# Weight conversion in a retention + two-MLP kernel: and-or on VectorE replaced by a parametric ReLU on ScalarE

## The chip, the cores and the metric

The kernel runs on one core of a Trainium2 chip. The metric is the device time of one execution in microseconds (us). Engine names are those of the profile: PE is TensorE's matrix multiplication, PEld its weight load, DVE is VectorE, ACT is ScalarE, POOL is GpSimd, SP issues the transfers. L127 is line 127 of the kernel before.

## The reference

Three stages follow each other. The first is a decayed attention without softmax (retention): 4 batches, 8 heads, 576 tokens, 64 dims a head. Its result is laid out as x of 2304 tokens by 512. Two MLPs of width 2048 follow, with different activations:

```python
scores = scale * np.matmul(q, k.transpose(0, 1, 3, 2))
out = np.matmul(scores * Dmat, v)          # Dmat: gamma[h] ** (i - j) for i >= j
h = np.maximum(x @ moe_w_in, 0.0)
x = h * h @ moe_w_out
h = x @ moe2_w_in
out = (h * np.clip(h + 3.0, 0.0, 6.0) / 6.0) @ moe2_w_out
```

The q, k, v are float32; the weights (512 x 2048 and 2048 x 512, twice) reach the kernel as the bits of float64 numbers, so that the kernel has to make float32 of them.

## The kernel before

**Numbers.** Each operand of the MLPs' products is held in two float32r parts, a high one and the rest, and a product is three matmuls: high times high, rest times high, high times rest.

**Weights.** A step of an MLP takes 128 of the 2048 inner columns, f = 0 to 15. Its weights are two halves, (f, 0) of w_in and (f, 1) of w_out, each a tile of 128 partitions by 512 float64. A half goes through four functions. `load_w` brings the raw words. `scale_w` is two ACT instructions: L109 multiplies the high word, read as a float32, by 2^-112, L110 multiplies the low word by 2^-29 and rounds it to an integer. `narrow_w` makes the float32 of them: L124 shifts the scaled high word three bits to the left (DVE), L125 puts back the sign bit, which the shift has lost (one DVE instruction that ands and ors), L127 adds the low word as an integer. L127 runs on DVE, but on POOL for the second halves of the second MLP. `split_w` makes the two parts: a rounding copy, L138 on ACT or L136 on DVE (`on_dve`), and a subtraction on POOL, L139.

**Steps.** `h_part` computes h for one block of tokens and one f: 12 matmuls (L296) into a PSUM tile `hp`, then the activation, then the two parts of g. In the first MLP ACT takes the ReLU of `hp` into r (L306); the square is ACT's L308 in block 0 and DVE's L310 (r times r) in the other blocks. The high part of g is ACT's L316 in block 0, DVE's L318 elsewhere; the rest is DVE's L319. In the second MLP the activation is L312 on ACT and L313 on DVE, which reads `hp` again. `a_part` adds g's product with w_out to the block's PSUM accumulators (L340 in the first MLP, L342 in the second) and evicts them after f = 15 (L363 DVE, L365 ACT). On PE the order is h of step i+1, then the retention's matmuls of step i, then a of step i. `hp` has two buffers.

**Order.** The order of each engine's instructions is written out by hand, and each engine takes them in that order. Blocks of the first MLP have 512, 384, 512, 384, 512 tokens, those of the second 384, 512, 512, 512, 384. First comes the retention of the first block's four chunks of 128 tokens, with the first weights between them. During block 0 every step narrows half (f+1, 1), splits half (f+2, 0) with ACT and half (f+1, 1) with DVE, computes h of f+1, narrows (f+3, 0) and scales two more halves on ACT. A chunk of the next block's retention is spread over four steps of every block of the first MLP but the last: `prep_chunk` (POOL L190), `scores` (PE L204, DVE L210), `values` (PE, DVE L246, ACT L249, POOL L250) and `states` (PE, DVE L276, POOL L277). The second MLP's 32 halves are converted from step 4 of the last block of the first MLP to the 15th of the second MLP's first block, one half a step, and two halves in each of five of these steps; scaling is done two steps ahead of splitting, narrowing one. In f = 8 to 11 of the block before, `load_x1` reads a second-MLP block's input (DVE L384, POOL L385).

Of the kernel before, what the change touches and what calls it, by code (L numbers as in the profile page):

```python
# [9 lines left out]
F32 = mybir.dt.float32  # L10
# [4 lines left out]
AF = mybir.ActivationFunctionType  # L15
ALU = mybir.AluOpType

P = 128
B, H, S, D = 4, 8, 576, 64
# [6 lines left out]
NCHUNK = NT // P  # L26
# Blocks of tokens of the first MLP and of the second, with the buffer that each one's input is in.
BLOCKS = (
# [3 lines left out]

# Columns of the table of constants.
VD0 = 0
# [6 lines left out]
def constants():  # L41
    """Decay factors and causal masks, by the shapes alone.

    Within a chunk of 128 tokens gamma^(i-j) / sqrt(D) is (gamma^(i+1) / sqrt(D)) for the query
    i times gamma^-(j+1) for the key j; the state of the chunks before takes gamma^128 a chunk.
    """
    gamma = 1.0 - 2.0 ** (-5.0 - np.arange(H, dtype=np.float64))
    t = np.arange(P, dtype=np.float64)
    c = np.zeros((P, NCONST), np.float64)
    for p in range(NPAIR):  # L50
        for e in range(2):
            g = gamma[2 * p + e]
            c[64 * e : 64 * e + 64, QD0 + p * P : QD0 + (p + 1) * P] = g ** (t + 1) / np.sqrt(D)
            c[64 * e : 64 * e + 64, GC0 + p] = g**P
    c[:, VD0 : VD0 + H] = gamma[None, :] ** -(t[:, None] + 1)
    causal = t[:, None] <= t[None, :]
    half = (t[:, None] < 64) == (t[None, :] < 64)
    c[:, MK0 : MK0 + P] = causal
    c[:, MK0 + P : MK0 + 2 * P] = causal & half
    return c.astype(np.float32)  # L60
# [3 lines left out]
def retention_moe_kernel(ctx: ExitStack, tc, qk, kv, w1, w2, cst, out):  # L64
    """qk [18, 128, 2, 512]: per chunk of 128 tokens q and k, by (head pair's dims; pair, token).
    kv [18, 128, 2, 512]: per chunk k and v, by (token; head, dim).
    w1, w2 [16, 128, 1024]: per 128 of d_ff w_in (dim within c; c, ff) and w_out (ff; dim), the
    64 bits of float64 numbers.
    """
    nc = tc.nc  # L70
# [19 lines left out]

# [1 line left out]
    raws = {}  # L92
    wts = {}

    def load_w(ph, f, halves=(0, 1)):
        """The raw numbers, into the room that their two parts will have, which is as large."""
        src = (w1, w2)[ph].bitcast(I32)
        for i in halves:
            t = wpool.tile([P, DM, 2], I32, tag=f"w{f}_{i}", name=f"raw_{ph}_{f}_{i}")
            nc.sync.dma_start(  # L100
                t, src[f, :, 2 * DM * i : 2 * DM * (i + 1)].rearrange("p (n t) -> p n t", t=2)
            )
            raws[ph, f, i] = t

    def scale_w(ph, f, halves=(0, 1)):
        for i in halves:
            raw = raws[ph, f, i]
            low, high = raw[:, :, 0], raw[:, :, 1]
            nc.scalar.activation(high.bitcast(F32), high.bitcast(F32), AF.Copy, scale=2.0**-112)  # L109
            nc.scalar.activation(low, low.bitcast(U32), AF.Copy, scale=2.0**-29)  # L110

    def narrow_w(ph, f, halves=(0, 1)):
        """float64 bits to float32, rounded to nearest.

        The high word, times 2^-112 as a float32, has its exponent rebased: three bits to the left
        it is the float32 truncated to 20 bits of fraction, but for the sign. The low word's top
        bits, rounded, are added to the word as an integer.
        """
        for i in halves:
            raw = raws.pop((ph, f, i))  # L120
            low, high = raw[:, :, 0], raw[:, :, 1]
            t = stg.tile([P, DM], F32, tag="wt", name=f"wt_{ph}_{f}_{i}")
            ti = t.bitcast(I32)
            nc.vector.tensor_scalar(ti, high, 3, None, ALU.logical_shift_left)  # L124
            nc.vector.scalar_tensor_tensor(ti, high, -(2**31), ti, ALU.bitwise_and, ALU.bitwise_or)  # L125
            eng = nc.gpsimd if ph and i else nc.vector
            eng.tensor_tensor(ti, ti, low, ALU.add)  # L127
            wts[ph, f, i] = t

    def split_w(ph, f, halves=(0, 1), on_dve=False):  # L130
        """float32 into two float32r parts."""
        for i in halves:
            t = wts[ph, f, i]
            w = wpool.tile([P, 2, DM], F32R, tag=f"w{f}_{i}", name=f"w_{ph}_{f}_{i}")
            if on_dve:
                nc.vector.tensor_copy(w[:, 0, :], t)  # L136
            else:
                nc.scalar.activation(w[:, 0, :], t, AF.Copy)  # L138
            nc.gpsimd.tensor_tensor(w[:, 1, :], t, w[:, 0, :].bitcast(F32), ALU.subtract)  # L139
            wts[ph, f, i] = w  # L140

# [1 line left out]
    con = apool.tile([P, NCONST], F32, tag="con", name="con")  # L143
# [3 lines left out]
    state = [apool.tile([P, NPAIR, P], F32, tag=f"s{i}", name=f"state{i}") for i in range(2)]  # L147

    # k by the head pair's dims, one head's at a time, with noughts in place of the other head's.
    # While the weights are not all there, two more chunks have room in their place.  # L150
    kts = [apool.tile([P, 2, NPAIR, P], F32, tag=f"kt{i}", name=f"kt{i}") for i in range(2)]
# [31 lines left out]
    def where(c):  # L183
        """Fresh: a batch begins with the chunk. Straddle: one ends in its middle."""
        t0 = c * P
        return t0 % S == 0, t0 // S != (t0 + P - 1) // S, (t0 + P) % S == 0
# [91 lines left out]

# [1 line left out]
    x1 = dpool.tile([P, NC, NT], F32, tag="x1", name="x1")  # L280
# [4 lines left out]
    def h_part(ph, blk, f):  # L285
# [4 lines left out]
        order = [(c, wi, xi) for wi, xi in ((0, 0), (1, 0), (0, 1)) for c in range(NC)]  # L290
        # The first half of the first block's tokens is there before the second.
        parts = 2 if ph == blk == f == 0 else 1
# [11 lines left out]
        r = r[:, :nb]  # L304
        if ph == 0:
            nc.scalar.activation(r, hp[:, :nb], AF.Relu)  # L306
            if blk == 0:
                nc.scalar.activation(r, r, AF.Square)  # L308
            else:
                nc.vector.tensor_tensor(r, r, r, ALU.mult)  # L310
        else:
            nc.scalar.activation(r, hp[:, :nb], AF.Relu, bias=con3)  # L312
            nc.vector.scalar_tensor_tensor(r, r, 6.0, hp[:, :nb], ALU.min, ALU.mult)  # L313
# [72 lines left out]

# [1 line left out]
    for t in state:  # L388
# [51 lines left out]

    # The second MLP's weights are split over the steps of two blocks, as the first one's make room.
    todo = {}
# [89 lines left out]
```

## Time and profile before

| | before |
|---|---|
| timed runs, us | 928.20, 926.77, 928.01 (median 928.01) |
| span of the profiled execution, first to last instruction | 924.4 us |
| instructions | 11741 |
| PE busy | 891.0 us, 96% of the span |
| DVE busy, instructions | 499.9 us, 772 |
| ACT busy, instructions | 240.3 us, 411 |
| POOL busy, instructions | 205.9 us, 169 |

The profiled execution has no time of its own beside its span; the median of the runs is 3.6 us longer than the span, which is what lies around the first and last instruction. Busy time of an engine is the union of its instructions' times. A PE that is busy is not at its full rate, since matmuls that wait for an operand inside a group stretch; the rate is read from the starts of groups of twelve matmuls.

### The profile page before, as it was taken

How to read it: one execution, taken by the hardware profiler on the slowest of the kernel's cores; microseconds unless marked ns; L12 is line 12 of the kernel's file. 1: busy time of each engine (PE TensorE's matmuls, PEld its weight loads, DVE VectorE, ACT ScalarE, POOL GpSimd, SP SyncE). 2: the span in 40 equal slices, each digit the busy share in tenths (PEclk: the TensorE clock that was granted, in tenths of full speed). 3: DMA queues.
4: the chain of work that ended last, by engine and by line, in shares of the span. 5: the costliest groups of instructions: out<-in, count | busy, mean ns of one | idle time of the engine just before them, and what ended most of it. 6: DMA issues, size and time to landing. Idle time of an engine off the chain costs nothing.

```text
span 924.4 us, 11741 instructions
## 1 busy us (share of the span) xinstructions
PE 891.0 (96%) x4716; PEld 760.1 (82%) x4716; DVE 499.9 (54%) x772; ACT 240.3 (26%) x411; POOL 205.9 (22%) x169
## 2 busy tenths in 40 slices
PE   7899999999999999999999997899999999999998
PEld 6677768999888899998877786788888888888997
DVE  5899995433433334433889899633343334333333
ACT  2666662111111111112444553211111111111111
POOL 5555551110101001120356356300100110010000
PEclk9899999999999999999999999999999999999999
DMA  8934511121201111105565300100020002000100
GB/s 287 364 100 155 206 46 46 46 69 47 80 23 46 46 46 46 46 1 166 202 215 169 126 0 12 59 11 1 12 80 1 12 0 72 1 9 0 46 1 35
DMA packets 26549, 67.73 MB, mean 73 GB/s; under 512 B 3200, under 2 KB 5376, under 8 KB 26496
## 3 DMA queue, kind: packets, MB, share of 16 engines
q1 hardware_dynamic: 26496, 67.00, 21.2%
q8 instruction: 37, 0.61, 0.3%
q14 instruction: 16, 0.13, 0.0%
HBM read 57.55 MB, written 9.44 MB: 72 GB/s over the span
## 4 chain that ended last, share of the span: by engine, by line
PE 72%; DVE 17%; DMA 5%; issue 3%; ACT 2%; POOL 1%; SPq 1%; DVEq 0%; ACTq 0%; POOLq 0%
PE h L296 33%; PE acc L342 18%; PE acc L340 15%; DVE wt L127 4%; DVE wt L125 4%; DVE wt L124 3%; DVE g L319 2%; PE sc L204 2%; DMA raw<-w_dram 2%; DVE g L318 2%; DMA kt<-qk_dram 1%; PE o L223 1%; PE o L233 1%; ACT r L306 1%; DVE r L313 1%
## 5 line engine op out<-in xcount | busy, mean ns | idle before, releaser
L296 PE MATMUL h<-x,w 128*128 128x512 f32 (+2 forms) x1932 | 425.9, 368 | 5.3 <-ACT w L138 3.0
L296 PEld LDWEIGHTS h<-x,w 128*128 128x128 f32 x1932 | 352.3, 188 | 57.7 <-POOL w L139 5.7
L340 PE MATMUL acc<-g,w 128*128 128x512 f32 (+1 forms) x960 | 217.2, 373 | 5.1 <-POOL w L139 1.8
L342 PE MATMUL acc<-w,g 128*128 128x512 f32 x864 | 212.8, 393 | 9.1 <-DVE g L318 8.2
L342 PEld LDWEIGHTS acc<-w,g 128*128 128x128 f32 x864 | 160.8, 188 | 46.1 <-DVE g L318 9.8
L340 PEld LDWEIGHTS acc<-g,w 128*128 128x128 f32 x960 | 172.0, 188 | 31.6 <-POOL w L139 3.9
L313 DVE SCALAR_TENSOR_TENSOR r<-r,h 128x512 f32<-128x512 f32 (+1 forms) x80 | 50.7, 633 | 202.9 <-ACT r L312 202.9
L310 DVE TENSOR_TENSOR r<-r 128x384 f32<-128x384 f32 (+1 forms) x64 | 42.3, 662 | 173.0 <-ACT r L306 172.9
L312 ACT ACTIVATE r<-h,con 128x512 f32<-128x512 f32 (+1 forms) x80 | 51.5, 644 | 283.0 <-PE h L296 274.4
L319 DVE TENSOR_TENSOR g<-r,g 128x512 fp32r<-128x512 f32 (+1 forms) x160 | 120.7, 754 | 6.3 <-ACT g L316 1.3
L139 POOL TENSOR_TENSOR w<-wt,w 128x512 fp32r<-128x512 f32 x64 | 96.4, 1510 | 82.3 <-ACT w L138 48.8
L306 ACT ACTIVATE r<-h 128x512 f32<-128x512 f32 (+1 forms) x80 | 44.1, 551 | 240.5 <-PE h L296 231.4
L318 DVE CAST g<-r 128x512 fp32r<-128x512 f32 (+1 forms) x144 | 71.6, 497 | 14.3
L385 POOL TENSOR_TENSOR x<-x1r,x 128x512 fp32r<-128x512 f32 (+1 forms) x20 | 25.4, 1271 | 240.1 <-DVE x L384 238.4
L250 POOL TENSOR_TENSOR x<-x,x 128x512 fp32r<-128x512 f32 (+1 forms) x19 | 23.6, 1245 | 208.7 <-ACT x L249 208.7
L125 DVE SCALAR_TENSOR_TENSOR wt<-raw,wt 128x512 int32<-128x512 int32 x64 | 58.3, 911 | 2.2
L138 ACT ACTIVATE w<-wt 128x512 fp32r<-128x512 f32 x48 | 30.3, 631 | 87.4 <-DVE wt L127 53.4
L127 DVE CUSTOM_DVE_ANT_0 wt<-raw,wt 128x1024 uint16<-128x1024 uint16 x48 | 46.9, 977 | 3.5
L204 PE MATMUL sc<-q,kt 128*128 128x128 f32 x288 | 38.0, 285 | 5.8 <-POOL kt L392 4.2
L204 PEld LDWEIGHTS sc<-q,kt 128*128 128x128 f32 x288 | 36.4, 199 | 7.4 <-POOL kt L392 4.2
L109 ACT ACTIVATE raw<-raw 128x512 f32<-128x512 f32 x64 | 42.5, 663 | 0.0
L110 ACT ACTIVATE raw<-raw 128x512 int32<-128x512 uint32 x64 | 42.4, 662 | 0.0
(33 smaller groups left out, 325.0 us busy)
## 6 DMA issues: line engine op xcount, KB each, us to landing
raw<-w_dram SPq DMA_DIRECT2D x64, 512.0 KB, 6.0
kv<-kv_dram SPq DMA_DIRECT2D x14, 512.0 KB, 3.2
q<-qk_dram SPq DMA_DIRECT2D x18, 256.0 KB, 2.9
kt<-qk_dram SPq DMA_DIRECT2D x36, 128.0 KB, 3.1
out_dram<-ev SPq DMA_DIRECT2D x18, 256.0 KB, 2.3
x<-ev SPq DMA_DIRECT2D x12, 256.0 KB, 2.1
x1r<-x SPq DMA_DIRECT2D x12, 256.0 KB, 3.5
kv<-kv_dram SPq DMA_DIRECT2D x8, 256.0 KB, 5.4
```

Source lines behind the costliest of these rows:

```text
L125: nc.vector.scalar_tensor_tensor(ti, high, -(2**31), ti, ALU.bitwise_and, ALU.bitwise_or)
L127: eng.tensor_tensor(ti, ti, low, ALU.add)
L139: nc.gpsimd.tensor_tensor(w[:, 1, :], t, w[:, 0, :].bitcast(F32), ALU.subtract)
L204: nc.tensor.matmul(sc[e][:, p, :], kt[:, e, p, :], q[:, p, :], start=True, stop=True)
L296: nc.tensor.matmul(hp[:, ts], w[:, wi, c * P : (c + 1) * P], x[:, xi, c, ts], start=k == 0, stop=k == 3 * NC - 1,)
L306: nc.scalar.activation(r, hp[:, :nb], AF.Relu)
L312: nc.scalar.activation(r, hp[:, :nb], AF.Relu, bias=con3)
L313: nc.vector.scalar_tensor_tensor(r, r, 6.0, hp[:, :nb], ALU.min, ALU.mult)
L318: nc.vector.tensor_copy(g[:, 0, :nb], r)
L319: nc.vector.tensor_tensor(g[:, 1, :nb], r, g[:, 0, :nb].bitcast(F32), ALU.subtract)
L340: nc.tensor.matmul(acc[d][:, :nb], wt[:, sl], gt, start=first, stop=stop)
L342: nc.tensor.matmul(acc[d], gt[:, sl], wt, start=first, stop=stop)
```

## The change

The multiplication of the high word on ACT becomes a parametric ReLU with the same scale and a slope of -(2^32) for negative numbers. A negative word comes out positive with an exponent that is 32 higher, and the shift by three carries that bit to the sign's place. L125 goes. The integer addition is on DVE in all 64 conversions. In the first MLP r becomes the ReLU times `hp`, on DVE, in all five blocks. The comments are taken out, with empty lines in their place.

```diff
-            nc.scalar.activation(high.bitcast(F32), high.bitcast(F32), AF.Copy, scale=2.0**-112)
+            high = high.bitcast(F32)
+            nc.scalar.activation(high, high, AF.Prelu, scale=2.0**-112, alpha=-(2.0**32))
             nc.scalar.activation(low, low.bitcast(U32), AF.Copy, scale=2.0**-29)
...
             nc.vector.tensor_scalar(ti, high, 3, None, ALU.logical_shift_left)
-            nc.vector.scalar_tensor_tensor(ti, high, -(2**31), ti, ALU.bitwise_and, ALU.bitwise_or)
-            eng = nc.gpsimd if ph and i else nc.vector
-            eng.tensor_tensor(ti, ti, low, ALU.add)
+            nc.vector.tensor_tensor(ti, ti, low, ALU.add)
...
             nc.scalar.activation(r, hp[:, :nb], AF.Relu)
-            if blk == 0:
-                nc.scalar.activation(r, r, AF.Square)
-            else:
-                nc.vector.tensor_tensor(r, r, r, ALU.mult)
+            nc.vector.tensor_tensor(r, r, hp[:, :nb], ALU.mult)
```

## Rows read from the trace of the kernel before

**Rows 1.** The page's second part: busy tenths of PE and DVE in 40 equal slices of the span (23.1 us each).

```profile
PE   7899999999999999999999997899999999999998
DVE  5899995433433334433889899633343334333333
```

**Rows 2.** Busy time by stage: block 0 of the first MLP, and the stretch in which the second MLP's weights are converted. Columns: stretch, its length, busy us (and instructions) of PE, PEld, DVE, ACT, POOL, then granted clock, DMA share, GB/s.

```profile
45.00:139.00 94.00, 89.48 (x477) 68.81 (x476) 90.08 (x119) 59.25 (x102) 51.53 (x36) 1.00 0.37 128
480.00:591.00 111.00, 96.23 (x437) 79.17 (x436) 102.77 (x130) 50.46 (x90) 60.82 (x43) 0.98 0.23 75
```

**Rows 3.** PE's timeline where nothing holds it up (start us, us, what): three steps of block 1, which carry one chunk of retention between them, and one step without; a step of 512 tokens of the first MLP; a step of 384 tokens of the second.

```profile
152.80 2.24 PE L296 MATMUL h<-x,w 128*128 128x384 f32 x12
...
170.04 2.24 PE L296 MATMUL h<-x,w 128*128 128x384 f32 x12
...
174.20 2.24 PE L296 MATMUL h<-x,w 128*128 128x384 f32 x12
...
430.58 2.88 PE L296 MATMUL h<-x,w 128*128 128x512 f32 x12
...
436.02 2.88 PE L296 MATMUL h<-x,w 128*128 128x512 f32 x12
...
525.90 2.27 PE L296 MATMUL h<-x,w 128*128 128x384 f32 x12
...
530.08 2.27 PE L296 MATMUL h<-x,w 128*128 128x384 f32 x12
```

**Rows 4.** PE's timeline at the ends of the two stretches: a of block 0's first step, h of block 1's first step; h of step 12 of the first MLP's last block, h of the second MLP's second block, first step.

```profile
38.66 3.02 PE L340 MATMUL acc<-g,w 128*128 128x512 f32 x12 [0.74 <-ACT g L316]
...
143.74 2.27 PE L296 MATMUL h<-x,w 128*128 128x384 f32 x12
...
479.54 2.88 PE L296 MATMUL h<-x,w 128*128 128x512 f32 x12
...
590.44 2.88 PE L296 MATMUL h<-x,w 128*128 128x512 f32 x12
```

**Rows 5.** Instructions grouped by line from 45 to 139 us. Columns: line, engine, operation, output<-inputs, shapes, count | busy us, mean ns | idle of the engine before them.

```profile
L127 DVE CUSTOM_DVE_ANT_0 wt<-raw,wt 128x1024 uint16<-128x1024 uint16 x26 | 29.9, 1152 | 2.3
L125 DVE SCALAR_TENSOR_TENSOR wt<-raw,wt 128x512 int32<-128x512 int32 x26 | 23.8, 916 | 0.9
L124 DVE TENSOR_SCALAR wt<-raw 128x512 int32<-128x512 int32 x26 | 17.4, 668 | 0.1
```

**Rows 6.** The same view from 480 to 591 us.

```profile
L125 DVE SCALAR_TENSOR_TENSOR wt<-raw,wt 128x512 int32<-128x512 int32 x24 | 21.6, 898 | 0.8
L319 DVE TENSOR_TENSOR g<-r,g 128x384 fp32r<-128x384 f32 x15 | 19.2, 1280 | 0.5
L127 POOL TENSOR_TENSOR wt<-wt,raw 128x512 int32<-128x512 int32 x12 | 16.9, 1404 | 19.9 <-DVE wt L125 16.6 <-issue 3.4
L124 DVE TENSOR_SCALAR wt<-raw 128x512 int32<-128x512 int32 x23 | 15.1, 655 | 0.0
L318 DVE CAST g<-r 128x384 fp32r<-128x384 f32 x16 | 12.6, 790 | 1.6
L127 DVE CUSTOM_DVE_ANT_0 wt<-raw,wt 128x1024 uint16<-128x1024 uint16 x12 | 8.3, 692 | 0.4
```

**Rows 7.** What these operations take where POOL doesn't work beside them: two lines of the view of one source line (duration ns min/median/max), two instructions of the last block from the timeline, and two groups over the whole span.

```profile
L124 DVE TENSOR_SCALAR wt<-raw x64: 410/420/1524, 19.1 to 585.6; 128x512 int32<-128x512 int32 x64
...
L125 DVE SCALAR_TENSOR_TENSOR wt<-raw,wt x64: 691/693/1781, 19.6 to 586.1; 128x512 int32<-128x512 int32 x64
...
909.56 0.36 DVE L318 CAST g<-r 128x384 fp32r<-128x384 f32 x1
...
909.95 0.56 DVE L319 TENSOR_TENSOR g<-r,g 128x384 fp32r<-128x384 f32 x1
...
L310 DVE TENSOR_TENSOR r<-r 128x384 f32<-128x384 f32 x32 | 17.9, 558 | 91.7 <-ACT r L306 91.7
...
L313 DVE SCALAR_TENSOR_TENSOR r<-r,h 128x384 f32<-128x384 f32 x32 | 17.6, 551 | 44.0 <-ACT r L312 44.0
```

**Rows 8.** The timeline of one step of block 0.

```profile
78.67 1.48 POOL L139 TENSOR_TENSOR w<-wt,w 128x512 fp32r<-128x512 f32 x1 [2.02 <-ACT w L138]
...
79.13 1.56 DVE L127 CUSTOM_DVE_ANT_0 wt<-raw,wt 128x1024 uint16<-128x1024 uint16 x1
...
79.78 0.63 ACT L316 ACTIVATE g<-r 128x512 fp32r<-128x512 f32 x1
...
81.08 0.68 DVE L319 TENSOR_TENSOR g<-r,g 128x512 fp32r<-128x512 f32 x1
```

**Rows 9.** The timeline of the first 32 us: the last DVE instruction of the first conversion, PE's wait for the retention's state, the first matmuls of the MLP.

```profile
21.13 1.54 DVE L127 CUSTOM_DVE_ANT_0 wt<-raw,wt 128x1024 uint16<-128x1024 uint16 x1
...
26.35 1.12 PE L223 MATMUL o<-p,kv 128*64 128x128 f32 x8 [3.31 <-DVE state L276]
...
31.82 6.11 PE L296 MATMUL h<-x,w 128*128 128x256 f32 x36
```

**Rows 10.** Busy time in two short stretches (columns as in Rows 2; the granted clock is the first figure behind the last bracket).

```profile
26.00:28.00 2.00, 1.65 (x11) 1.35 (x11) 1.90 (x4) 0.66 (x2) 1.26 (x2) 0.50 1.02 407
586.00:588.00 2.00, 2.00 (x8) 2.00 (x7) 0.74 (x2) 0.00 (x0) 1.15 (x1) 0.50 0.00 0
```

**Rows 11.** The only table load of the whole span, in the view by line.

```profile
L243 ACT ACT_TABLE_LOAD x1 | 1.3, 1283 | 0.7 <-PEq L521 0.7
```

## The prediction

> **What bounds the kernel now.** I read the page's slices first [rows 1]. PE is at 9 in nearly all of them; the slices below 9 are the first two and those around slices 22 to 25, and there DVE is at 8 or 9. Everywhere else DVE is at 3 to 5. So the time is PE's own work plus what DVE takes from it in three places: the start, block 0, and the conversion of the second MLP's weights. The view by stage [rows 2] confirms it: DVE is busy 90.1 of 94 us in block 0 and 102.8 of 111 us in the second stretch, while ACT has 59 and 50 and POOL 52 and 61.
>
> PE's busy share hides the loss, so I take it from starts of matmul groups [rows 3]. Undisturbed, a 512-token step of the first MLP takes 436.02 - 430.58 = 5.44 us (2.72 for h, as much for a), a step of 384 tokens of the second 530.08 - 525.90 = 4.18, one of the first MLP 174.20 - 170.04 = 4.16. A chunk of retention adds (170.04 - 152.80) - 3 x 4.16 = 4.8 us. Block 0, from its first a to block 1's first h, holds 31 halves of a step and three chunks: 31 x 2.72 + 3 x 4.8 = 98.6 us. It takes 143.74 - 38.66 = 105.1 [rows 4], so 6.5 us are lost. From 479.54 to 590.44 there are four steps of 5.44, the change of blocks (h of 384 tokens, half of 4.16, and a of 512: 2.08 + 2.72) and fifteen steps of 4.18: 89.3 us. It takes 110.9; 21.6 us are lost. These two sums are the most that each stretch can give back.
>
> A second thing sets DVE's pace. In [rows 8] L127 begins at 79.13, while POOL's L139 runs from 78.67 to 80.15, and takes 1.56 us; the same operation takes 0.69 in the other stretch, where it never meets one [rows 6]. L124 has a minimum of 0.41 and a maximum of 1.52, L125 0.69 and 1.78 [rows 7]. A DVE instruction that works on SBUF alone waits until POOL's is done. The excess over the undisturbed time in block 0 is 26 x (1.152 - 0.692) = 12.0 us for L127, 26 x (0.916 - 0.693) = 5.8 for L125 and 26 x (0.668 - 0.42) = 6.4 for L124 [rows 5, 7]: 24 us for 51.5 us of POOL's work, 0.47 us for each. In the second stretch L125, L124, L318 and L319 give 4.9 + 5.4 + 6.9 + 10.8 = 28 us [rows 6, 7] for 60.8, or 0.46. So an instruction taken from POOL gives DVE nearly half of its time back.
>
> **The change, part by part.**
>
> *L125 away, everywhere.* Each costs DVE 0.69 us; the wait for POOL that it may have held passes to the next instruction, and I count that as not saved.
>
> *The addition for sixteen halves moves from POOL to DVE.* Twelve lie in the second stretch. DVE takes 12 x 0.692 = 8.3 us more; POOL loses 16.9 us [rows 6], which at 0.46 returns 7.8 us of waits. With L125 gone (24 x 0.69 = 16.6) DVE's demand there falls by 16.6 - 8.3 + 7.8 = 16 us, and it sets the pace for nearly the whole stretch. Its 111 us would become 95, still above PE's 89.3. Bounds of the gain: all of PE's loss, 21.6, above, and 6 below, if the waits remain that come from two halves or an input piece in one step. I take 14, a little under DVE's own 16: in the three steps with two halves DVE still needs more than 4.18 us (0.55 + 0.36 + 0.56 for the activation, 2 x 1.1 for the conversions, 0.46 x 2 x 1.4 of waits: 5.0). The conversion's path to PE also loses POOL's 1.4 us and one change of engine before L138.
>
> *Block 0: L125 away, the square moved to DVE.* From 45 to 139 us DVE loses 26 x 0.69 = 17.9 us and gains 13 multiplications (26 conversions are 13 steps). These read PSUM and SBUF like L313, which at 384 columns takes 0.551 against 0.558 for L310, which reads SBUF alone [rows 7]; so 0.69 at 512, 9.0 together, and no wait for POOL. Net -8.9 us. But r now goes ACT, DVE, ACT, DVE where it stayed on ACT for three instructions: DVE's next instruction is L319, and it waits for L316, 0.63 us on ACT [rows 8] and some 0.1 us of signalling. Nothing stands between them in DVE's order, so DVE stands still 0.7 us a step, 13 x 0.7 = 9.1 us. Behind it wait the next conversion's L124 and the retention's L210, L246 and L276; behind L316 on ACT wait four scalings and the next L138. Bounds: if the standstill falls into time in which POOL's L139 would have held up L124 anyway (6.4 us of such waits), DVE falls to some 94 - 8.9 + 2.7 = 88 us, which is PE's share of these 94 us (98.6 x 94 / 105.1 = 88.2), and all 6.5 us come back; if it adds in full, 94 - 8.9 + 9.1 = 94, and nothing does. I take the middle, 3.5. The next bound then is PE in steps with retention and ACT's order in the others.
>
> [...]
>
> *Blocks 1 to 4 of the first MLP.* L310 reads `hp` in place of r: the same time, PE hides it (DVE at 3 to 4 tenths, rows 1). `hp` is freed after DVE's instruction instead of ACT's; PE's next use of that buffer comes after a, which needs that DVE result anyway. Nothing.
>
> *The start.* DVE's instructions between 19 and 31 us are in one queue with the retention: PE waits 3.31 us for the state at 26.35, behind the first conversion, whose L127 runs till 22.67, and begins h at 31.82 [rows 9]. Two L125 stand ahead of that h, each between 0.69 and 1.78 us. PE also runs at half its clock behind that wait (0.50 from 26 to 28 us, rows 10), so a shorter wait may save a little more. Bounds 0 and 4 us; I take 2.5, two L125 at a mid value.
>
> *The parametric ReLU itself.* The trace has none. I take it to cost what the multiplication cost; ACT has 35 of 94 us free in block 0, and loses the square. That it costs more, by a table load, is the first rival.
>
> Sum: 2.5 + 3.5 + 14 = 20 us off the span of 924.4, so 904.4; with the 3.6 us around it 908.0, against the median of 928.01.
>
> **Rivals.**
>
> *Table loads (slower).* If the parametric ReLU lies in another table set than the copy beside it, ACT loads a table before and after each: 1.283 us [rows 11]. Place: `scale_w`, two halves a step in block 0, so four loads, 5.1 us. The 94 us hold 13 steps (26 conversions), of 7.2 us, and ACT is busy for 59.25 / 13 = 4.6 of them; less the square and with the loads it is 9.1: 1.9 us a step over now, 28 in fifteen. In the second stretch 24 x 2 x 1.283 = 62 us come to ACT's 50, about its length: nothing gained. With some 5 us at the start 928 + 33 = 961. It decides from two loads a step on, where ACT (4.0 + 2.6) passes PE's 98.6 / 15.5 = 6.4 us. For it: only one load in the whole span shows, and no such function. Against: that one load serves ReLU, square and copy together. Chance 0.05.
>
> [...]
>
> *The round trip costs more than it frees (slower).* In block 0, if each standstill also sets L319 behind a POOL instruction (0.87 as in rows 8) and L316's lateness delays L138 and so PE's next weights by 0.6, a step has 0.69 + 0.7 + 0.87 + 0.6 - 1.38 = 1.5 us more: 22 us, against 16.5 gained elsewhere: 933. It decides from 1.1 us a step. DVE's fullness speaks for it; against it, POOL's L139 for the DVE-split half runs just during the standstill. Chance 0.05.
>
> *A milder form of it.* Half a microsecond a step, +7.5 in place of -3.5: 919, still faster. Chance 0.14.
>
> *The second stretch keeps its waits.* The steps with two halves or an input piece lose what they lose now, and 6 us come back: 916. For it: DVE's order is fixed, and most PE waits sit in such steps. Chance 0.15.
>
> *Both of the last two and no gain at the start.* 928 + 7.5 - 6, less if PE's clock falls after a longer wait as it did at 586 us [rows 10]: about no change. Chance 0.04.
>
> **Numbers.** Forecast 908.0, chance 0.57, its own range 901 to 915. Faster by over 0.2% (what a measurement of this kernel can tell from none): 0.57 + 0.14 + 0.15 = 0.86; the same 0.04; slower 0.10. With every bound at its best the time is 928 - 4 - 6.5 - 21.6 = 896; I cut that to 900, since the three don't come together, and reach up to 921 to hold the two milder rivals.
>
> **What would show it.** L125 is gone and DVE's count falls by 64 - 16 - 16 = 32. From 480 us on, the second stretch shortens from 110.9 to about 97 us and DVE is no longer full in single steps; block 0 takes about 101.5, with DVE idle before L319 some 0.7 us, ended by ACT's L316; h begins near 29.5. It is wrong if ACT shows more than one table load, if block 0 takes more than 105, or if PE still waits over 10 us for L318 and w after 480 us.

## The result and the profile after

The changed kernel takes 901.61 us (median of four runs, 900.91 to 902.37). The kernel before, with one more run beside it, takes 927.53 (926.77 to 928.20): 25.9 us less, where the forecast was 20 less and 908.0. The ratio on record is 0.9726, 95% interval 0.9712 to 0.974 (the two medians alone give 0.972).

The first parts of the page after, instruction counts and slices of 22.5 us (compare rows 1):

```profile
span 898.8 us, 11669 instructions
PE 882.0 (98%) x4716; PEld 760.8 (85%) x4716; DVE 455.5 (51%) x740; ACT 229.8 (26%) x395; POOL 174.2 (19%) x153
...
PE   7899999999999999999999999999999999999998
...
DVE  4888884343343343443679899433333333333333
```

DVE has 32 instructions fewer and is busy for 455.5 us where it was for 499.9, ACT for 229.8 (240.3), POOL for 174.2 (205.9). PE's slices below 9 around the second MLP's weights have gone. DVE is still at 8 or 9 in slices 2 to 6 and 22 to 25, the same two places.

Some lines move in the new file: the high word's scaling is L110 (was L109), the shift L126 (L124), ReLU times `hp` L307, the high part of g L313 on ACT (L316) and L315 on DVE (L318), its rest L316 (L319), `a_part` L337 and L339 (L340, L342), the second MLP's activation L309 and L310.

PE's timeline after, at the ends of the stages (start us, us, what; compare rows 4): first a of block 0, first h of block 1, h of step 12 of the first MLP's last block, first h of the second MLP's second block.

```profile
36.93 2.94 PE L337 MATMUL acc<-g,w 128*128 128x512 f32 x12
...
134.91 2.27 PE L296 MATMUL h<-x,w 128*128 128x384 f32 x12
...
470.71 2.88 PE L296 MATMUL h<-x,w 128*128 128x512 f32 x12
...
564.77 2.88 PE L296 MATMUL h<-x,w 128*128 128x512 f32 x12
```

The differences between such starts give the stages. Block 0 is 134.91 - 36.93 = 98.0 us where it was 105.1, the second stretch 564.77 - 470.71 = 94.1 where it was 110.9, and the first a comes 1.7 us earlier: 7.1 + 16.8 + 1.7 = 25.6, the whole difference of the spans (924.4 - 898.8). Between the two stretches (335.8 us) and after the second (334.0) nothing changed.

Busy time in both stretches after (columns as in rows 2):

```profile
43.00:132.00 89.00, 87.21 (x478) 69.94 (x477) 75.14 (x107) 53.56 (x95) 46.49 (x36) 1.00 0.42 147
470.00:565.00 95.00, 92.33 (x441) 79.45 (x439) 85.06 (x119) 51.40 (x90) 40.55 (x31) 1.00 0.27 90
```

DVE has fallen from 96% of block 0 to 75.1 of 89 us, and from 102.8 of 111 to 85.1 of 95. The table loads that a rival feared did not come; over the whole span the view by line has one, as before, and the parametric ReLU takes what the scaled copy took (first line: the scaled copy in the kernel before, whole span; then two lines after):

```profile
L109 ACT ACTIVATE raw<-raw 128x512 f32<-128x512 f32 x64 | 42.5, 663 | 0.0
...
L110 ACT ACTIVATE raw<-raw 128x512 f32<-128x512 f32 x64 | 42.5, 664 | 0.0
...
L243 ACT ACT_TABLE_LOAD x1 | 1.3, 1283 | 0.7 <-PEq L518 0.7
```

### The profile page after: what moved, and what is told of

Same layout as the page of the kernel before. It is cut to its first block, busy times and chain, and to the rows that moved or that the text cites. A ratio compares the mean times of both kernels' runs of the same rounds, so it can differ in the third digit from the quotient of the medians.

```text
span 898.8 us, 11669 instructions
## 1 busy us (share of the span) xinstructions
PE 882.0 (98%) x4716; PEld 760.8 (85%) x4716; DVE 455.5 (51%) x740; ACT 229.8 (26%) x395; POOL 174.2 (19%) x153
## 4 chain that ended last, share of the span: by engine, by line
PE 82%; DMA 6%; DVE 5%; issue 3%; ACT 1%; POOL 1%; SPq 1%; DVEq 0%; POOLq 0%; ACTq 0%
PE h L296 38%; PE acc L339 20%; PE acc L337 18%; PE sc L204 2%; DMA raw<-w_dram 2%; DMA kv<-kv_dram 2%; PE o L223 2%; PE o L233 2%; DVE g L315 1%; DVE wt L127 1%; POOL w L139 1%; DVE wt L126 1%; DMA q<-qk_dram 1%; PE st L262 1%; DVE r L307 1%
## 5 line engine op out<-in xcount | busy, mean ns | idle before, releaser
L337 PE MATMUL acc<-g,w 128*128 128x512 f32 (+1 forms) x960 | 214.8, 372 | 0.0
L339 PE MATMUL acc<-w,g 128*128 128x512 f32 x864 | 210.9, 391 | 1.5 <-DVE g L315 1.5
L337 PEld LDWEIGHTS acc<-g,w 128*128 128x128 f32 x960 | 172.7, 188 | 22.7 <-ACT g L313 0.2
L339 PEld LDWEIGHTS acc<-w,g 128*128 128x128 f32 x864 | 161.1, 188 | 35.7 <-DVE g L315 2.6
L310 DVE SCALAR_TENSOR_TENSOR r<-r,h 128x512 f32<-128x512 f32 (+1 forms) x80 | 50.8, 634 | 203.0 <-ACT r L309 203.0
L307 DVE TENSOR_TENSOR r<-r,h 128x512 f32<-128x512 f32 (+1 forms) x80 | 50.6, 633 | 177.7 <-ACT r L306 177.6
L316 DVE TENSOR_TENSOR g<-r,g 128x512 fp32r<-128x512 f32 (+1 forms) x160 | 123.6, 772 | 16.2 <-ACT g L313 11.2
L309 ACT ACTIVATE r<-h,con 128x512 f32<-128x512 f32 (+1 forms) x80 | 51.7, 647 | 295.2 <-PE h L296 283.6
L139 POOL TENSOR_TENSOR w<-wt,w 128x512 fp32r<-128x512 f32 x64 | 88.3, 1386 | 125.4 <-ACT w L138 100.0
L306 ACT ACTIVATE r<-h 128x512 f32<-128x512 f32 (+1 forms) x80 | 44.3, 553 | 249.4 <-PE h L296 244.7
L315 DVE CAST g<-r 128x512 fp32r<-128x512 f32 (+1 forms) x144 | 72.3, 502 | 14.6 <-DVE r L310 0.5
L382 POOL TENSOR_TENSOR x<-x1r,x 128x512 fp32r<-128x512 f32 (+1 forms) x20 | 23.6, 1182 | 252.1 <-DVE x L381 249.5
L127 DVE CUSTOM_DVE_ANT_0 wt<-raw,wt 128x1024 uint16<-128x1024 uint16 x64 | 46.9, 733 | 4.4 <-ACT raw L111 0.6
L204 PE MATMUL sc<-q,kt 128*128 128x128 f32 x288 | 38.7, 291 | 6.3 <-DMA kt<-qk_dram 6.3
L110 ACT ACTIVATE raw<-raw 128x512 f32<-128x512 f32 x64 | 42.5, 664 | 0.0
L126 DVE TENSOR_SCALAR wt<-raw 128x512 int32<-128x512 int32 x64 | 33.2, 518 | 1.0 <-ACT raw L110 0.8
```

Source lines behind the costliest of these rows:

```text
L127: nc.vector.tensor_tensor(ti, ti, low, ALU.add)
L204: nc.tensor.matmul(sc[e][:, p, :], kt[:, e, p, :], q[:, p, :], start=True, stop=True)
L307: nc.vector.tensor_tensor(r, r, hp[:, :nb], ALU.mult)
L315: nc.vector.tensor_copy(g[:, 0, :nb], r)
L316: nc.vector.tensor_tensor(g[:, 1, :nb], r, g[:, 0, :nb].bitcast(F32), ALU.subtract)
L337: nc.tensor.matmul(acc[d][:, :nb], wt[:, sl], gt, start=first, stop=stop)
```

## The experiments

Every kernel was read at the same four starts: the first a of block 0 ("first a" in the table), the first h of block 1, h of step 12 of the first MLP's last block, and the first h of the second MLP's second block. All times are in us; the medians are of four runs, but of one each for the two repeats. The stage between the stretches was 335.8 to 336.2 in all of them, the one after 334.0 to 334.3.

| kernel | first a | block 0 | second stretch | median | ratio to before (95%) |
|---|---|---|---|---|---|
| before | 38.7 | 105.1 | 110.9 | 927.53 | |
| after | 36.9 | 98.0 | 94.1 | 901.61 | 0.9726 (0.9712 to 0.974) |
| square alone (e1) | 39.4 | 116.0 | 107.8 | 934.77 | 1.0093 (1.0067 to 1.0118) |
| sign alone (e2) | 37.9 | 93.3 | 94.9 | 897.10 | 0.9681 (0.9661 to 0.9701) |
| after, block 0's square on ACT (e3) | 38.9 | 93.3 | 94.1 | 897.34 | 0.9682 (0.966 to 0.9703) |
| after, subtractions on DVE (e4) | 38.4 | 102.6 | 90.7 | 903.83 | 0.9744 (0.9715 to 0.9773) |
| after, block 0's copy of g on DVE (e5) | 37.0 | 101.1 | 94.1 | 905.27 | 0.9757 (0.9742 to 0.9773) |
| e3 with e4 in the second MLP (e6) | 36.3 | 93.3 | 90.7 | 891.81 | 0.9621 (0.9594 to 0.9649) |
| after, other places of the halves (e7) | 37.0 | 97.6 | 94.2 | 901.57 | 0.9719 (0.9701 to 0.9738) |
| before, again (e8) | 40.6 | 105.0 | 110.6 | 928.29 | |
| after, again (e9) | 39.2 | 97.7 | 94.0 | 902.84 | |

**Square alone (e1).** The kernel before, with nothing changed but the square:

```diff
-            if blk == 0:
-                nc.scalar.activation(r, r, AF.Square)
-            else:
-                nc.vector.tensor_tensor(r, r, r, ALU.mult)
+            nc.vector.tensor_tensor(r, r, hp[:, :nb], ALU.mult)
```

> The kernel before, with the square alone moved: the ReLU times h on DVE in all five blocks of the first MLP; the and-or and POOL's additions stay. Block 0 (first a of block 0 to the first h of block 1) took 105.1 us before. Theory O, by which DVE's standstill for ACT's rounding copy falls into time in which POOL's subtraction would have held DVE up anyway: a step gains a multiplication of 0.69 us and little else, so block 0 takes 105 + 14.5 x 0.75 = 116 us and the kernel 938. Theory A, by which the standstill adds in full: 0.69 + 0.7 a step, block 0 takes 125 us and the kernel 947. If PE had room for both, nothing would change (928); DVE's 90 busy us of 94 speak against it.

Block 0 took 116.0, 10.9 more than before, as theory O had it; the kernel is 0.9% slower, its interval clear of 1. The view by line of this kernel, 45 to 150 us (columns as in rows 5), and its view of waits (waiting line <- releaser: us in total, times, longest); from L306 on its lines are numbered as in the changed file:

```profile
L127 DVE CUSTOM_DVE_ANT_0 wt<-raw,wt 128x1024 uint16<-128x1024 uint16 x27 | 32.9, 1218 | 2.3
L125 DVE SCALAR_TENSOR_TENSOR wt<-raw,wt 128x512 int32<-128x512 int32 x26 | 18.6, 715 | 0.9
L124 DVE TENSOR_SCALAR wt<-raw 128x512 int32<-128x512 int32 x26 | 11.8, 455 | 0.1
L316 DVE TENSOR_TENSOR g<-r,g 128x512 fp32r<-128x512 f32 x13 | 10.6, 817 | 9.1 <-ACT g L313 9.1
L307 DVE TENSOR_TENSOR r<-r,h 128x512 f32<-128x512 f32 x13 | 8.9, 682 | 0.1
```

```profile
ACT g L313 <- DVE r L307: 38.4, 13, 6.3
...
DVE g L316 <- ACT g L313: 9.1, 13, 0.7
```

These lines make up the sum. DVE has 8.9 us of products and stands still for 9.1 (0.70 a step, as forecast), and ACT waits for a product up to 6.3 us at a time. DVE's waits for POOL, counted as mean less the time alone, are 27 x (1218 - 692) + 26 x (715 - 693) + 26 x (455 - 420) + 13 x (817 - 693) ns = 17.3 us, where before had 24: 7 us less. 8.9 + 9.1 - 7 = 11.0, the 10.9 measured. (693 is what the rest of g takes alone, in e4.) The waits shrink because a subtraction of POOL's now falls into the product and the standstill. The timeline of one step shows it: DVE stands still from 78.83 to 79.53, and POOL's subtraction runs from 78.19 to 79.48.

```profile
78.14 0.69 DVE L307 TENSOR_TENSOR r<-r,h 128x512 f32<-128x512 f32 x1
...
78.19 1.29 POOL L139 TENSOR_TENSOR w<-wt,w 128x512 fp32r<-128x512 f32 x1 [1.09 <-DVE w L136]
...
79.53 1.50 DVE L316 TENSOR_TENSOR g<-r,g 128x512 fp32r<-128x512 f32 x1 [0.70 <-ACT g L313]
```

Added up over the timelines of the 13 steps, POOL is at work in 9.0 of the 9.1 us of standstill.

In the second stretch the same edit gained 3.1 us, which is why the kernel stayed 3 us below theory O's 938. Five multiplications of the first MLP's last steps lie there, and their mean fell from 907 ns (r times r, both in SBUF, POOL beside it) to 679 with `hp` in PSUM, 1.1 us of the 3.1 by itself; the rest is not traced. The line of before (480 to 591 us) and the line of this kernel (491 to 599):

```profile
L310 DVE TENSOR_TENSOR r<-r 128x512 f32<-128x512 f32 x5 | 4.5, 907 | 0.0
...
L307 DVE TENSOR_TENSOR r<-r,h 128x512 f32<-128x512 f32 x5 | 3.4, 679 | 0.0
```

**Sign alone (e2).** The kernel before with the parametric ReLU and without L125; the square and POOL's additions stay:

```diff
-            nc.scalar.activation(high.bitcast(F32), high.bitcast(F32), AF.Copy, scale=2.0**-112)
+            high = high.bitcast(F32)
+            nc.scalar.activation(high, high, AF.Prelu, scale=2.0**-112, alpha=-(2.0**32))
...
-            nc.vector.scalar_tensor_tensor(ti, high, -(2**31), ti, ALU.bitwise_and, ALU.bitwise_or)
```

> The kernel before, with the parametric ReLU and without the and-or alone; POOL's sixteen additions and ACT's square stay. By the prediction's own accounting the move of the additions is worth nothing to DVE (8.3 us more work, 7.8 us of waits for POOL less), so the second stretch (470.7 to 564.8 us in the changed kernel, 94.1 us) should take 94 to 96 us here too, block 0 98, and the kernel 902 to 904. Rival P: what PE waited for was the path of a half through POOL (1.4 us and a change of engine between DVE and ACT's rounding copy); then the second stretch keeps some 8 us of its waits, takes 102 or more, and the kernel 910 or more.

897.10: this part alone is 4.5 us faster than the whole change. It takes block 0 to 93.3, where 98 was expected, and the kernel stays 5 us below the 902 to 904 expected, for a reason given in the next part; the second stretch, at 94.9, came as expected. What the whole change adds to it in that stretch, the additions on DVE and the product with `hp` in the first MLP's last steps, is worth 0.86 us together (94.92 to 94.06).

**The change with block 0's square back on ACT (e3).**

```diff
-            nc.vector.tensor_tensor(r, r, hp[:, :nb], ALU.mult)
+            if blk == 0:
+                nc.scalar.activation(r, r, AF.Square)
+            else:
+                nc.vector.tensor_tensor(r, r, hp[:, :nb], ALU.mult)
```

> The changed kernel, with block 0's square back on ACT, so that r stays on ACT for three instructions and DVE doesn't stand still before the subtraction for g. Theory O and the bound by PE: block 0 is at PE's rate already, so it takes 97 to 99 us as in the changed kernel and the time is the same within 1.5 us (900 to 903). If the round trip still costs something behind PE's back, block 0 gets shorter by up to 1 or 2 us. If ACT's square were the worse place (ACT's scalings later), it gets longer by 1 us or more.

93.3 again, and 4.3 us faster than the changed kernel (897.34 against 901.61). Expected was no difference beyond 1 or 2 us, since block 0 was thought to be at PE's rate already; it was not. Busy time (columns as in rows 2) and waits from 43 to 128 us; here L316 and L319 are ACT's copy of g and its rest, as in the file before:

```profile
43.00:128.00 85.00, 85.00 (x481) 70.25 (x480) 73.12 (x96) 61.82 (x106) 51.07 (x37) 1.00 0.44 158
```

```profile
DVE g L319 <- ACT g L316: 7.9, 7, 2.5
...
ACT r L306 <- PE h L296: 4.9, 6, 1.3
```

PE is busy in all of it and ACT waits for PE's h: PE sets the pace. DVE still stands still for ACT's copy of g, for 7.9 us, and it costs nothing there.

**The changed kernel with all 64 subtractions on DVE (e4).**

```diff
-            nc.gpsimd.tensor_tensor(w[:, 1, :], t, w[:, 0, :].bitcast(F32), ALU.subtract)
+            nc.vector.tensor_tensor(w[:, 1, :], t, w[:, 0, :].bitcast(F32), ALU.subtract)
```

> The changed kernel, with the weights' 64 subtractions on DVE in place of POOL: 0.69 us more DVE work for each, 17.9 us in block 0 and 16.6 in the second stretch. Theory L, by which DVE's long instructions wait for POOL: the same instructions lose about as much in waits (17 us in block 0, over 20 in the second stretch, counted as mean less undisturbed time in the changed kernel), so both stretches stay within 4 us of the changed kernel's, and the kernel takes 898 to 907; DVE's instructions are near their undisturbed times wherever POOL is idle. Rival, by which the long instructions have another cause than POOL (transfers, ACT): DVE gets 34 us of work more in two stretches where it has some 10 to spare, and the kernel takes 920 or more, with the long instructions as long as before.

The two stretches go opposite ways. The second falls to 90.7. The same lines by the view by line, over the second stretch from start to start, first of the changed kernel (470.71 to 564.77 us), then of this one (476.77 to 567.48), and the busy time of both (columns as in rows 2):

```profile
L316 DVE TENSOR_TENSOR g<-r,g 128x384 fp32r<-128x384 f32 x15 | 19.1, 1275 | 0.5
...
L315 DVE CAST g<-r 128x384 fp32r<-128x384 f32 x16 | 14.1, 883 | 1.9 <-DVE r L310 0.5
```

```profile
L139 DVE TENSOR_TENSOR w<-wt,w 128x512 fp32r<-128x512 f32 x23 | 15.5, 685 | 0.0
...
L316 DVE TENSOR_TENSOR g<-r,g 128x384 fp32r<-128x384 f32 x16 | 8.9, 559 | 0.6
...
L315 DVE CAST g<-r 128x384 fp32r<-128x384 f32 x16 | 8.6, 539 | 1.6
```

```profile
470.71:564.77 94.06, 91.39 (x436) 78.70 (x435) 84.16 (x118) 51.40 (x90) 40.32 (x31) 1.00 0.27 89
...
476.77:567.48 90.71, 89.97 (x437) 79.15 (x436) 76.25 (x141) 50.03 (x89) 8.28 (x7) 1.00 0.28 93
```

DVE takes on 15.5 us of work and is busy for 76.3 us instead of 84.2: L316 falls from 1275 to 559 ns, L315 from 883 to 539. There POOL's subtraction had cost DVE more than doing it. In block 0 it does not pay, 102.6 against 98.0. The view by line, 43 to 138 us:

```profile
L127 DVE CUSTOM_DVE_ANT_0 wt<-raw,wt 128x1024 uint16<-128x1024 uint16 x26 | 19.2, 739 | 2.7 <-ACT w L138 0.5
L139 DVE TENSOR_TENSOR w<-wt,w 128x512 fp32r<-128x512 f32 x27 | 18.6, 689 | 1.6 <-ACT w L138 0.9
L126 DVE TENSOR_SCALAR wt<-raw 128x512 int32<-128x512 int32 x26 | 15.2, 583 | 0.7 <-ACT raw L110 0.6
...
L316 DVE TENSOR_TENSOR g<-r,g 128x512 fp32r<-128x512 f32 x13 | 9.0, 693 | 9.1 <-ACT g L313 9.1
```

DVE has 27 x 689 ns = 18.6 us more of its own. Of its waits for POOL, 17.2 us in the changed kernel (worked out in the next part), L127 at 739 ns and L126 at 583 still hold 26 x (739 - 692) + 26 x (583 - 420) ns = 5.4, so 11.8 came back: 6.8 us more for DVE by these sums, and a block that is 4.6 longer. (Instructions overlap a little at their ends, by up to 0.09 us in the changed kernel's timeline; DVE's busy time over the block, which counts an overlap once, rose by 4.3 us, from 82.9 to 87.2.) The standstill stays, 9.1 us. In the changed kernel POOL worked in 9.0 of these 9.1 us, by the timelines of both engines, so that much of its subtraction had cost DVE nothing.

**The changed kernel with block 0's copy of g on DVE (e5).** No wait for ACT is then left between two DVE instructions of the activation:

```diff
-        if ph == 0 and blk == 0:
-            nc.scalar.activation(g[:, 0, :nb], r, AF.Copy)
-        else:
-            nc.vector.tensor_copy(g[:, 0, :nb], r)
+        nc.vector.tensor_copy(g[:, 0, :nb], r)
```

> The changed kernel, with block 0's rounding copy of g (L313) on DVE instead of ACT, so that r doesn't go back to ACT: ACT, DVE, DVE, DVE. In the changed kernel block 0 takes 98.0 us, 4.7 more than with the square on ACT (93.3). Theory S, by which those 4.7 us are DVE's standstill for ACT's copy (9.8 us in 14 steps): the standstill goes, DVE gets 14 x 0.43 = 6.0 us of copies, 3.8 less in all, and block 0 takes 93 to 95, the kernel 897 to 899. Theory M, by which the standstill lies beside POOL's work and costs nothing and the 4.7 us are the multiplication's time on DVE: the copies come on top, and block 0 takes 101 to 104, the kernel 905 to 908.

Block 0 grew to 101.1 and the kernel to 905.27, as theory M had it; theory S's 93 to 95 did not come. In the view by line, 45 to 138 us, the standstill is gone, but the copy L312 takes 825 ns, where a copy of this shape takes 427 without POOL beside it (L136 in block 0 before), and the rest of g, L313, 1028, where it took 960:

```profile
L313 DVE TENSOR_TENSOR g<-r,g 128x512 fp32r<-128x512 f32 x13 | 13.4, 1028 | 0.5
...
L312 DVE CAST g<-r 128x512 fp32r<-128x512 f32 x13 | 10.7, 825 | 1.3
```

**Both good halves together (e6).** e3's edit, and the subtraction on DVE for the second MLP alone:

```diff
-            nc.gpsimd.tensor_tensor(w[:, 1, :], t, w[:, 0, :].bitcast(F32), ALU.subtract)
+            eng = nc.vector if ph else nc.gpsimd
+            eng.tensor_tensor(w[:, 1, :], t, w[:, 0, :].bitcast(F32), ALU.subtract)
```

> The changed kernel with block 0's square on ACT, and with the subtractions on DVE for the second MLP's weights alone (on POOL for the first's). If the two effects seen apart add up: block 0 93.3 as with the square on ACT, the second stretch 90.7 as with all subtractions on DVE (PE's own work there is 89.3), and the kernel 897.3 - 3.4 = 894, faster than any before. If they don't, because the longer path on ACT in block 0 or a later start shifts the second stretch, 896 to 898.

891.81, faster than both kernels of the study by 35.1 (926.87 beside it) and 9.8 us. The stretches are those of e3 and e4, 93.3 and 90.7, so the two edits add. It came out 2 us below the 894 expected; in its profiled execution the first a came 2.6 us earlier than in e3's, and the start varies by about as much from one execution of a kernel to the next (e8, e9).

**Other places for the second MLP's halves (e7).** Two halves a step in eight steps of the first MLP's last block, four of them right before the change of blocks, then one a step, and the input pieces of the next block three steps later:

```diff
-        todo.setdefault(4 + n * 27 // (2 * NF), []).append(n)
+        todo.setdefault(when[n], []).append(n)
...
-        if ph == 1 and blk + 1 < nblk and 8 <= f < 8 + NC:
-            load_x1(blk + 1, f - 8)
+        if ph == 1 and blk + 1 < nblk and 11 <= f < 11 + NC:
+            load_x1(blk + 1, f - 11)
```

where `when` is `[4,4,5,5,6,6,7,7,8,9,10,11,12,12,13,13,14,14,15,15] + list(range(16, 28))`.

> The changed kernel with another plan of the second MLP's conversions, and nothing else: two halves in eight of the steps of the first MLP's last block (5.44 us of PE work each), then one in each of the steps 0 to 11 of the second MLP's first block (4.18 us each), and the input pieces of the next block read in steps 11 to 14, behind the last conversions. By the prediction's account the 4.8 us that the second stretch still loses (94.1 against PE's 89.3) sit in steps with two halves or with an input piece; then the stretch falls to 90 to 91.5 and the kernel to 898. Rival: DVE and POOL are too full in the steps with two halves of the last block, and PE waits there instead; the stretch and what lies ahead of it stay at 94 or get longer, and the kernel is at 901 or more.

94.2: the same, as the rival had it. PE's timeline shows where it went. In this kernel the steps with input pieces run at 4.18 us from 508 on, but PE now waits around the change of blocks:

```profile
494.75 0.73 PE L337 MATMUL acc<-g,w 128*128 128x512 f32 x2 [0.16 <-DVE g L315]
...
496.44 2.57 PE L337 MATMUL acc<-g,w 128*128 128x512 f32 x10 [0.96 <-DVE g L316]
...
502.21 0.73 PE L339 MATMUL acc<-w,g 128*128 128x512 f32 x2 [0.56 <-ACT ev L362]
...
508.03 2.37 PE L339 MATMUL acc<-w,g 128*128 128x512 f32 x9 [1.30 <-DVE g L315]
```

**Both kernels profiled again (e8, e9).** Nothing is edited; they tell how far a stage repeats.

> The kernel before, unchanged, profiled a second time, for the start alone: its first a began at 38.66 us, 20.5 us after the scores of chunk 3 (18.20). If the start's loss is DVE's queue and the arrival of inputs only shifts it, the 20.5 us come again within 1 us, whatever the scores' own start; block 0 takes 105 and the second stretch 111 again. If the arrival of inputs decides, the 20.5 us change by more than 1 us.

> The changed kernel, unchanged, profiled a second time, for the start alone: from the scores of chunk 3 to the first a it took 17.2 us. If DVE's queue sets it, 17 to 18 us come again, some 3 less than before; block 0 takes 98 and the second stretch 94 again. If the arrival of inputs decides, the two kernels overlap here.

The stretches repeat within 0.4 us. The start does not: the first a came at 40.6 and 39.2, 1.9 and 2.3 us later than in the first profiles, and the intervals from the fourth chunk's scores, 19.1 and 18.9 us, missed the 20.5 and the 17 to 18 that DVE's queue alone would have given.

## Why the prediction was right, and where its steps were not

The time lies in the range, on the side and by the mechanism that was forecast, 6.4 us below the point and 1.6 above the range's lower end. That it lies inside is in part luck: a gain that the forecast had ruled out (block 0 below 98.6) came with e2's edit, which alone takes 897.10 and would have left the range, and the square took 4.7 us of it back.

Of the 6.4, 0.8 is the difference between the median and the span of the profiled execution (2.8 us here, not 3.6). That difference is not only what lies around the first and last instruction: in the runs on record a run's time is 1.8 to 2.2 us above its own span, and the rest is how the profiled execution differed from the median one. The other 5.6 are the three terms below.

**Start: 2.5 forecast, 1.7 in the profiles.** It can't be told closer, and one sign of it did not come: h began at 31.21 us, where 29.5 was forecast and 31.82 was measured before. From the scores of the fourth chunk to the first a it took 20.5 and 19.1 us in the two profiles of before, 17.2 and 18.9 in those of after. The three profiles with the and-or have their first a at 39.5 us on the mean, the eight profiles without it at 37.7. The sign and about 2 us stand on the means, though single kernels overlap (39.2 in e9, 38.7 in before); how much of it is the and-or and how much the arrival of the inputs stays open.

**Block 0: 3.5 forecast, of at most 6.5; 7.1 measured.** The step that failed is the floor, "31 halves of a step and three chunks". On PE, h of a step stands ahead of the a of the step before. From the first a to the next block's first h there are then fifteen a and fourteen h, 29 halves: 29 x 2.72 + 3 x 4.8 = 93.3. Three kernels run at just that (93.3 in e2, e3 and e6), so 98.6 was no floor at all, and before had lost 11.8 us, not 6.5.

The case that the forecast had for its upper gain was near the mark; its cap of 6.5 and the middle were not. Without L125 alone all 11.8 come back (e2); moving the square gives 4.7 of them away (98.0 against e3's 93.3). The forecast had this as one of its two cases, DVE at 88 of 94 us, which is 88 x 105.1 / 94 = 98.4 for the block, and took a middle between it and no gain. That 98.4 and the false floor of 98.6 nearly agree is chance. The view by line of the changed kernel, 43 to 132 us, answers to rows 5; in front of it, from the view of rows 5, L136 before:

```profile
L136 DVE CAST w<-wt 128x512 fp32r<-128x512 f32 x13 | 5.6, 427 | 0.4
...
L127 DVE CUSTOM_DVE_ANT_0 wt<-raw,wt 128x1024 uint16<-128x1024 uint16 x26 | 18.6, 715 | 2.7 <-ACT raw L111 0.6
L136 DVE CAST w<-wt 128x512 fp32r<-128x512 f32 x13 | 15.3, 1175 | 0.4
L126 DVE TENSOR_SCALAR wt<-raw 128x512 int32<-128x512 int32 x26 | 14.1, 541 | 0.9 <-ACT raw L110 0.8
L316 DVE TENSOR_TENSOR g<-r,g 128x512 fp32r<-128x512 f32 x14 | 13.4, 960 | 9.8 <-ACT g L313 9.8
L307 DVE TENSOR_TENSOR r<-r,h 128x512 f32<-128x512 f32 x13 | 8.9, 681 | 0.6 <-ACT r L306 0.5
```

The standstill was sized right, 9.8 us in 14 steps, ended by ACT's copy of g. It does not add in full, since waits for POOL shrink beside it as in e1, by 7 us, where that case had put 6.4: 26 x (715 - 692) + 26 x (541 - 420) + 13 x (1175 - 427) + 14 x (960 - 693) ns = 17.2 us (alone: rows 6 and 7, 427 for L136, and 693 for L316 in e4). They also changed places: the subtraction that held up L127 (1152 ns) now holds up L136 (427 before, 1175 after) and the rest of g. By e1's sum, 17.9 of L125 and 7 of waits less against 8.9 of products and 9.8 of standstill more make 6.2 us less for DVE, near the 7.1 of the block: DVE still sets its pace, and in e4 and e5 more work for DVE made the block longer (102.6 and 101.1 against 98.0). e5 shows that the standstill is not the thing to remove: in its place comes work that waits.

**The multiplication itself: right.** "so 0.69 at 512" and "no wait for POOL" came out at 681 ns in a block in which POOL works half of the time; by the timelines 7.6 of the 8.9 us of L307 lie beside POOL's work, and none of its 80 instructions took more than 690 ns. L307 has its other input in PSUM; L316 and L136, which work on SBUF alone, take 267 and 748 ns more than alone in the same block. A source in PSUM cost nothing here: 128 x 384 took 555 ns with `hp` against 558 with r twice [rows 7]. Over the whole span:

```profile
L307 DVE TENSOR_TENSOR r<-r,h 128x512 f32<-128x512 f32 x48 | 32.9, 685 | 86.3 <-ACT r L306 86.2
L307 DVE TENSOR_TENSOR r<-r,h 128x384 f32<-128x384 f32 x32 | 17.7, 555 | 91.3 <-ACT r L306 91.3
```

**Second stretch: 14 forecast, 16.8 measured.** DVE's own fall, 16 us, was near: its busy time fell from 102.7 to 84.2 us between the same two starts, and e2 gains 16.0. What failed is the cut to 14 for "the three steps with two halves". PE's timeline after has no wait in them; one is a step of 512 tokens, for which 4.18 was the wrong measure, and they run at 5.44 and 4.18 us like the others of their length. The 94.06 - 89.3 = 4.8 us that are left lie at the change of blocks and in f = 11 to 14 of the second MLP's first block, right behind the four input pieces (f = 8 to 11):

```profile
504.57 2.34 PE L339 MATMUL acc<-w,g 128*128 128x512 f32 x9 [0.78 <-DVE g L315]
...
547.38 2.52 PE L339 MATMUL acc<-w,g 128*128 128x512 f32 x9 [0.68 <-DVE g L315]
...
559.84 0.96 PE L296 MATMUL h<-x,w 128*128 128x384 f32 x4 [0.82 <-ACT w L138]
```

The last pair of halves has a share in the wait at 547 that no run tells apart: DVE narrows it at 537.4 to 539.5 us, right ahead of the first input piece, and stands still nowhere from there to 555. Of the 4.8 us e4's edit returns 3.4 (90.7); e7 frees these steps of pairs and input pieces alike and pays as much at the change of blocks, where it crowds the halves. The additions on DVE, priced at 8.3 - 7.8 = 0.5 of loss, gained at most the 0.86 between e2 and the change: right as near nothing. The waits that this price rests on were undercounted: five instructions each of L318, L319 and L310 at 512 columns (means of 1172, 1469 and 907 ns in the view of rows 6) hold some 9 us more, 37 in place of 28 or 0.60 of POOL's time, which by itself would have made the additions a gain of about 2. (Nor do PE's slices in rows 1 fall below 9 at 22 to 25: it is 25, 26 and the last. Nothing rests on that.)

The rivals fall as follows: the table loads with the single load of 1283 ns, as before (that the parametric ReLU might need a table of its own was the forecast's supposition), the dear round trip and its milder form with 98.0 us in block 0, the waits that stay with 94.1 in the second stretch. The place of the round trip was real all the same, and where DVE has no room, in e1, it and the products cost 10.9 us and made that kernel slower.

A part of the second stretch's gain is the clock, which the forecast did not price there. Before, PE waited 2.64 us at the end of the stretch, the granted clock then fell to 0.50 [rows 10], and eight matmuls of h took 2.93 us. In the changed kernel PE waits 0.82 us at that place (559.84 above), the clock stays at 1.00, and the same eight take 1.66, so about 1.3 of the 16.8 us came this way. Two lines of before, one of after, and the busy time of after there:

```profile
584.00 0.98 PE L296 MATMUL h<-x,w 128*128 128x384 f32 x4 [2.64 <-ACT w L138]
585.35 2.93 PE L296 MATMUL h<-x,w 128*128 128x384 f32 x8 [0.38 <-POOL w L139]
...
561.19 1.66 PE L296 MATMUL h<-x,w 128*128 128x384 f32 x8 [0.39 <-POOL w L139]
...
558.00:562.00 4.00, 2.79 (x13) 1.94 (x13) 3.79 (x7) 0.63 (x1) 1.27 (x1) 1.00 0.00 0
```

## What to carry to other kernels

Count an engine's own work in the order in which it takes its groups, from the first mark to the last, before calling the rest a loss: two halves too many hid 5.4 us of gain here. A change that frees an engine and one that loads it should be judged apart, even when they come in one edit: here the first was worth 30 us, the rest took 4.5 back, and putting the square back and moving the subtraction where it pays gave 891.81. Price an instruction on POOL by its own time and by the waits that it imposes on DVE (0.60 of its time in the second stretch of before), and ask in each stage whether DVE would do it for less.

## What the runs showed of the hardware

The waits that POOL's work imposes on DVE can exceed what the moved work costs DVE: in the second stretch 23 subtractions of 685 ns came to DVE, and its busy time fell from 84.2 to 76.3 us. The same edit in block 0 returned 11.8 us of waits for 18.6 of work. What differs is where the subtraction falls: in block 0 9.0 us of POOL's work lie under DVE's standstill and 7.6 beside the product with `hp`, and that part of it holds up nothing. That this accounts for the whole difference between the stretches is my reading; no run changes the overlap alone. How long an instruction is held up, the timeline of before shows: in block 0 (45 to 139 us) the ten L124 that start while an instruction of POOL's runs take 0.62 to 1.52 us, against 0.42 alone, and each ends 0.27 to 0.29 us after POOL's. In the second stretch L316 at 384 columns takes 1275 ns in the changed kernel, with the subtractions on POOL, and 559 in e4. By what means POOL holds them up, no run shows.
